# A new order of the opening transfers: value weights in two transfers on SyncE's queue, the head map on ScalarE's

## The chip, the cores and the metric

The kernel runs on one core of a Trainium2 chip. The metric is the time of one execution in microseconds (us) of device time. The profile also gives a span, from the first to the last counted instruction; it is somewhat shorter than the time. SyncE, ScalarE (ACT) and GpSimd (POOL) issue transfers (DMAs); VectorE is DVE, TensorE is PE. "Landing" is the moment at which the last of a transfer's 16 completions is in, so that an instruction that waits for it may go (in the kernel before x's second half landed at 6.22 us, and the product that waited for it started at 6.27). Three runs of the kernel before gave 148.55 us as the median.

## The reference

The function mixes two blocks over x (2048 rows of 448, bf16), row by row, with a gate.

```python
g = sigmoid((x * gate_w).sum(-1, keepdims=True))
a = A(x)   # linear attention, 16 heads of 28: qkv = x @ wqkv; a head map w_phi on q and k,
           # softmax of it and of its negative; kv = phi_k^T v; o = phi_q kv / (phi_q z); o @ wo
b = B(x)   # gelu(x @ w1 + b1) @ w2 + b2, hidden size 1792
return g * a + (1 - g) * b
```

The kernel multiplies the head map into the key and query weights first ("fuse", tile `w_ps`), so that a key goes from x to its features in one product. That fuse needs the key weights transposed, and the map.

## The kernel before

Only the opening matters here. Transfers are issued in the order of these lines, each on the queue of the engine that is named:

```python
nc.vector.memset(warm[:], 0.0)
nc.vector.memset(wphi[HP:P, 3, :], 0.0)          # the map's unused rows alone (HP = 64, P = 128)
nc.vector.memset(gb[:], 0.0); nc.vector.memset(bb[:], 0.0)
nc.sync.dma_start(x0[:, 0:2, :], two[0])         # x, first half of its first 512 rows, 224 KB
nc.scalar.activation(out=tiny[:, 0:1], in_=warm[0:1, 0:1], func=ACT.Exp)
nc.scalar.dma_start(WvG[:, 0:3, 0:D], A_wqkv[0:384, 2 * D:3 * D].rearrange("(c p) n -> p c n", p=P))   # 336 KB
wflat = A_w_phi.rearrange("h a b -> (h a) b")
nc.sync.dma_start(wphi[:, 0:3, :], wflat[0:384, :].rearrange("(c p) b -> p c b", p=P))   # 21 KB
nc.scalar.dma_start(wphi[0:HP, 3, :], wflat[384:448, :])                                 # 3.5 KB
nc.sync.dma_start(x0[:, 2:4, :], two[1])         # x, second half, 224 KB
# ... GpSimd: the last 64 rows of the value weights twice (2 x 56 KB), gate weights, ...
load_wT(WkT, D, 0, 256)                          # key weights, transposing transfers on SyncE
load_wT(WkT, D, 256, D)
```

TensorE meanwhile runs filler products, turns x (`tp`), and multiplies by the value weights (`v_ps`):

```python
idle(5); idle(6, P)                              # fillers (w_warm)
turn(0, 1, nc.vector.tensor_copy, 0, 2)          # needs x's first half
turn(0, 2, nc.scalar.copy, 2, 4)
turn(2, 0, nc.vector.tensor_copy)
idle(2, P)
v0a, v0b = V(0, 3), V(1, 0)
v0a.un.full(0, True, False)                      # 3 products, one for each value chunk of 128 rows
v0a.un.full(1, True, False, cs=(0,))
# ... then the turns and products of x's second half, then the fuse of the key weights
```

The softmax here doesn't subtract the row's maximum and nothing guards it: scores larger than these inputs give would overflow.

## Time and profile before

| Kernel before | |
|---|---|
| time, span | 148.78 us and 147.1 us in the profiled run |
| x's first half: issue, landing | 0.80, 3.43 us |
| value weights (one transfer) | 0.96, 4.67 us |
| x's second half | 1.73, 6.22 us |
| key weights, two transposes: landing | 7.12, 8.44 us |
| first product of the key fuse (`w_ps`) | 8.33 us |

The page's first part says how busy each engine is; TensorE, at 97%, is the bound, so a change in the opening acts by when TensorE can run through without a hole. The moment that sums the opening up is the start of the first `w_ps` product, 8.33 us: from there to the end of the span it takes 138.8 us (147.1 - 8.33). The prediction below shows the lines of this profile with the chain of waits and the timeline up to 6.9 us. Two further lines of TensorE's timeline are needed for comparison (start, length, engine, line, operation, output and inputs, shape, count):

```profile
6.72 1.77 PE L194 MATMUL v_ps<-gel,xT 128*128 128x448 bf16 x8
8.33 0.63 PE L316 MATMUL w_ps<-gel 128*128 128x140 bf16 x8
```

Eight products of 448 columns take 1.77 us, and the fuse follows; single products of 448 columns start 0.19 us apart in the instruction records.

### The profile page before, as it was taken

What the parts mean: (1) busy time and instruction counts of PE and PEld (TensorE: products, weight loads), DVE (VectorE), ACT (ScalarE), POOL (GpSimd) and SP (SyncE); (2) the same over time, 40 slices, a digit from 0 to 9 for tenths busy, and PEclk for the clock granted to TensorE, in tenths of its full rate; (3) what the DMA queues carried; (4) which work ended last, traced back from release to release, by engine and by line L of the source; (5) the groups of instructions that cost most, each with busy time, mean ns of one, the idle gap of its engine ahead of it and who ended that gap; (6) DMA issues with size and microseconds to landing.
All of it is one profiled execution on the core that took longest, in us unless ns stands there. A gap on an engine that the chain in (4) does not pass through costs nothing.

```text
span 147.1 us, 3117 instructions
## 1 busy us (share of the span) xinstructions
PE 142.9 (97%) x1293; PEld 78.5 (53%) x1293; DVE 82.5 (56%) x140; ACT 64.8 (44%) x73; POOL 72.0 (49%) x59
## 2 busy tenths in 40 slices
PE   7899999999999999999999999999999999999992
PEld 4554645554566666964444445554555555545561
DVE  0342999997999992179993002721637747044112
ACT  4266987889999877326777762000000000000000
POOL 7932499898889999200699940000621110024000
PEclk9999999999999999999999999999999999999999
DMA  4999857449999999997159990340313623303111
GB/s 129 266 184 224 199 123 150 108 85 241 224 221 223 366 246 145 181 153 139 38 98 171 100 206 0 71 76 2 125 31 85 87 69 71 71 4 125 60 34 31
DMA packets 46190, 18.98 MB, mean 129 GB/s; under 512 B 36800, under 2 KB 46016, under 8 KB 46176
## 3 DMA queue, kind: packets, MB, share of 16 engines
q1 hardware_dynamic: 45392, 18.23, 61.8%
q10 hardware_dynamic: 624, 0.43, 0.9%
q8 instruction: 10, 0.16, 0.5%
q0 software_dynamic: 160, 0.12, 0.3%
q14 instruction: 4, 0.03, 0.1%
HBM read 6.34 MB, written 1.84 MB: 56 GB/s over the span
## 4 chain that ended last, share of the span: by engine, by line
PE 94%; DMA 3%; SPq 1%; DVE 0%; issue 0%
PE hp L478 29%; PE y L577 28%; PE q_ps L231 6%; PE y L194 6%; PE k_ps L231 4%; PE v_ps L194 3%; DMA gel<-in_A_x_dram 3%; PE v_ps L231 3%; PE kv L490 3%; PE nm L502 2%; PE k_ps L205 2%; PE k_ps L194 2%; PE w_ps L316 1%; PE y L211 1%; PE q_ps L194 1%; PE v_ps L211 1%
## 5 line engine op out<-in xcount | busy, mean ns | idle before, releaser
L577 PE MATMUL y<-w_sb,gel 128*128 128x448 bf16 (+1 forms) x224 | 43.8, 349 | 0.0
L478 PE MATMUL hp<-xT,w_sb 64*128 64x512 bf16 x224 | 42.7, 376 | 0.0
L478 PE MATMUL hp<-xS,w_sb 64*128 64x512 bf16 x168 | 40.1, 376 | 0.0
L482 ACT ACTIVATE gel<-hp,b1T 128x1024 bf16<-128x1024 f32 x28 | 30.8, 1115 | 13.6 <-PE hp L478 13.0
L478 PEld LDWEIGHTS <-w_sb 64*128 64x128 bf16 x392 | 22.9, 94 | 19.1
L577 PEld LDWEIGHTS <-gel 128*128 128x128 bf16 x238 | 22.3, 98 | 19.3 <-issue 0.4
L538 POOL TENSOR_SCALAR b2u<-b2b,ungate 128x448 f32<-128x448 bf16 x16 | 10.0, 642 | 40.2 <-DVE res L589 40.2
L259 POOL TENSOR_TENSOR gel<-gel,rec 128x1792 bf16<-128x1792 bf16 x8 | 25.6, 3214 | 2.2 <-DVE rec L258 2.2
L589 DVE SCALAR_TENSOR_TENSOR res<-y,ungate,b2u 128x448 bf16<-128x448 f32 (+1 forms) x16 | 10.3, 673 | 25.0 <-PE y L577 13.2
L259 POOL TENSOR_TENSOR phiq<-phiq,rec 128x1792 bf16<-128x1792 bf16 x4 | 12.7, 3211 | 11.0 <-DVE rec L258 11.0
L256 DVE TENSOR_REDUCE sums<-gel 128x64 f32<-128x1792 bf16 x8 | 16.0, 2002 | 0.0
L250 ACT ACTIVATE gel<-k_ps 128x896 bf16<-128x896 f32 x16 | 13.7, 922 | 3.5 <-PE k_ps L231 2.1
L509 DVE TENSOR_SCALAR den<-nm,enL 128x16 f32<-128x16 f32 x16 | 3.6, 228 | 17.0 <-PE nm L502 17.0
L231 PEld LDWEIGHTS <-xT 64*128 64x128 bf16 x112 | 9.2, 94 | 5.6 <-issue 0.4
L259 POOL TENSOR_TENSOR phqT<-phqT,rec 128x1792 bf16<-128x1792 bf16 x3 | 11.3, 3808 | 0.0
L515 DVE TENSOR_TENSOR o_all<-nm,den 128x448 bf16<-128x448 f32 (+2 forms) x24 | 11.0, 485 | 0.6
L231 PE MATMUL q_ps<-gel,xT 64*128 64x448 bf16 (+1 forms) x56 | 10.1, 349 | 0.0
L231 PEld LDWEIGHTS <-xS 64*128 64x128 bf16 x84 | 7.8, 94 | 3.8
L258 DVE RECIPROCAL rec<-sums 128x64 f32<-128x64 f32 x16 | 8.9, 553 | 1.1
L231 PE MATMUL q_ps<-phqT,xS 64*128 64x448 bf16 (+1 forms) x42 | 9.1, 349 | 0.0
L278 DVE CAST vaug<-v_ps 128x896 bf16<-128x896 f32 x7 | 7.5, 1070 | 2.7 <-PE v_ps L194 2.4
L194 PE MATMUL y<-wo_sb,phiq 128*128 128x448 bf16 (+1 forms) x36 | 8.2, 349 | 0.0
(96 smaller groups left out, 146.4 us busy)
## 6 DMA issues: line engine op xcount, KB each, us to landing
w_sb<-in_B_w_dram SPq DMA_DIRECT2D x4, 784.0 KB, 10.8
out_dram<-res SPq DMA_DIRECT2D x15, 112.0 KB, 1.7
w_sb<-in_B_w_dram SPq DMA_DIRECT2D x2, 560.0 KB, 13.6
xS<-xT SPq DMA_DIRECT2D x8, 96.0 KB, 2.3
phqT<-gel SPq DMA_DIRECT2D x4, 168.4 KB, 3.4
gel<-in_A_x_dram SPq DMA_DIRECT2D x2, 224.0 KB, 3.6
w_sb<-in_B_w_dram SPq DMA_DIRECT2D x1, 448.0 KB, 10.2
gel<-in_A_wqkv_dram ACTq DMA_DIRECT2D x1, 336.0 KB, 3.7
```

The source lines that it names most:

```text
L194: nc.tensor.matmul(o, lhsT=self.L(i, slice(0, P), c), rhs=self.R(slice(0, P), c)[:, n0:n1], start=(first and c == 0), stop=(last and c == 2))
L231: nc.tensor.matmul(o, lhsT=tok, rhs=(W if direct else SWAPPED[name])[rows, c, 0:n], start=(k == 0), stop=own)
L250: nc.scalar.activation(out=o, in_=src, func=ACT.Exp, scale=(1.0, -1.0)[s])
L256: nc.vector.reduce_sum(out=sums[:], in_=ph, axis=AX.X)
L258: nc.vector.reciprocal(out=rec[:], in_=sums[:])
L259: eng.tensor_tensor(out=ph, in0=ph, in1=rec[:, :, :, None].to_broadcast([P, 32, 2, DH]), op=ALU.mult)
L478: nc.tensor.matmul(hp[:, i, :].rearrange("p (b t) -> p b t", b=2), lhsT=w1_sb[i * HP:(i + 1) * HP, k, j * P:(j + 1) * P], rhs=x_half(i, k, ...
L482: nc.scalar.activation(out=dst, in_=hp[:].rearrange("p i (b t) -> p i b t", b=2), func=ACT.Gelu_apprx_tanh, bias=b1T[:, j:j + 1])
L515: nc.vector.tensor_tensor(out=o_tok[:, col:col + (b - a) * DH].rearrange("p (q j d) -> p q j d", j=2, d=DH), in0=nm[:, a // 2:b // 2, 0:56 ...
L538: nc.gpsimd.tensor_scalar(out=b2u[t][:], in0=b2b[:], scalar1=ungate[:, place(t):place(t) + 1], scalar2=0.0, op0=ALU.mult, op1=ALU.add)
L577: nc.tensor.matmul(o, lhsT=gel[:, j, tok], rhs=w2_sb[:, j, n0:n1], start=(first and j == 0), stop=(last and j == NJ - 1))
L589: nc.vector.scalar_tensor_tensor(out=res[t][:, n0:n1], in0=o, scalar=ungate[:, e:e + 1], in1=b2u[t][:, n0:n1], op0=ALU.mult, op1=ALU.add)
```

## The change

Its intent is to have the first value chunk sooner and to let x's and the value weights' bytes flow from one queue in the order in which TensorE wants them, with the small packets of the map out of the way on ScalarE's queue.

```diff
     nc.vector.memset(warm[:], 0.0)
-    nc.vector.memset(wphi[HP:P, 3, :], 0.0)
     nc.vector.memset(gb[:], 0.0)
     nc.vector.memset(bb[:], 0.0)
+    nc.vector.memset(wphi[:], 0.0)
     nc.sync.dma_start(x0[:, 0:2, :], two[0])
     nc.scalar.activation(out=tiny[:, 0:1], in_=warm[0:1, 0:1], func=ACT.Exp)
-    nc.scalar.dma_start(WvG[:, 0:3, 0:D], A_wqkv[0:384, 2 * D:3 * D].rearrange("(c p) n -> p c n", p=P))
+    for c0, c1 in ((0, 1), (1, 3)):
+        nc.sync.dma_start(WvG[:, c0:c1, 0:D],
+                          A_wqkv[c0 * P:c1 * P, 2 * D:3 * D].rearrange("(c p) n -> p c n", p=P))
+    nc.sync.dma_start(x0[:, 2:4, :], two[1])
     wflat = A_w_phi.rearrange("h a b -> (h a) b")
-    nc.sync.dma_start(wphi[:, 0:3, :], wflat[0:384, :].rearrange("(c p) b -> p c b", p=P))
+    nc.scalar.dma_start(wphi[:, 0:3, :], wflat[0:384, :].rearrange("(c p) b -> p c b", p=P))
     nc.scalar.dma_start(wphi[0:HP, 3, :], wflat[384:448, :])
-    nc.sync.dma_start(x0[:, 2:4, :], two[1])
 ...
-    for c0, c1 in ((0, 1), (1, 3)):
-        nc.sync.dma_start(wo_sb[:, c0:c1, :], A_wo[c0 * P:c1 * P, :].rearrange("(c p) n -> p c n", p=P))
+    nc.sync.dma_start(wo_sb[:, 0:3, :], A_wo[0:384, :].rearrange("(c p) n -> p c n", p=P))
```

The output weights in one transfer are a side effect: the number of transfers stays what it was.

## The prediction

> **What bounds the kernel now.** I read the page's first part first, then the chain of waits in order of time, then the timeline of the first 14 us, and last the landings of the transfers that the change touches.
>
> ```profile
> PE 142.9 (97%) x1293; PEld 78.5 (53%) x1293; DVE 82.5 (56%) x140; ACT 64.8 (44%) x73; POOL 72.0 (49%) x59
> ```
>
> TensorE is busy 142.9 of 147.1 us. Whatever the change does, it can only take from the 4.2 us in which TensorE is idle, or add to them. The chain in order of time says where those lie in the part that the change touches:
>
> ```profile
> 0.74 0.06 issue
> 0.80 0.41 SPq L116
> 1.21 0.06 issue
> 1.27 0.41 SPq L120
> 1.68 0.05 issue
> 1.73 4.49 DMA gel<-in_A_x_dram
> 6.22 0.05 issue
> 6.27 0.62 PE tp L336 x8
> 6.88 1.61 PE v_ps L194 x8
> ```
>
> The columns are start, length in us and what it was. The chain begins with three issues on SyncE (x's first half, the head map wphi, x's second half), then the flight of x's second half from 1.73 to 6.22 us, and from 6.27 us on it is TensorE piece by piece until the end. So the whole kernel starts at the landing of x's second half; what comes later or sooner at 6.22 us moves the end one for one, as long as no other transfer takes over. The timeline on TensorE shows how long it waits there:
>
> ```profile
> 3.57 1.06 PE L336 MATMUL tp<-ident,gel 128*128 128x128 bf16 x8
> 4.42 0.42 PE L322 MATMUL w_warm<-const-bfloat16-1.0 128*128 128x128 bf16 x2
> 4.89 0.93 PE L194 MATMUL v_ps<-gel,xT 128*128 128x448 bf16 x4
> 6.27 0.62 PE L336 MATMUL tp<-ident,gel 128*128 128x128 bf16 x8 [0.44 <-DMA gel<-in_A_x_dram]
> ```
>
> The page's idle is 0.44 us, from the modelled end of the fourth value matmul. In the instruction records these matmuls start 0.19 us apart (5.09, 5.28, 5.47), so the next one could have started at 5.66: the real hole before x's second half is 6.27 - 5.66 = 0.61 us. That is one limit of a gain. There is a second, smaller hole: the last filler starts at 4.53, fillers are 0.107 us apart, and the first value matmul comes at 4.89 instead of 4.63. The value weights landed at 4.67 and TensorE's sequencer ended its wait at 4.70, so 0.26 us are lost to the value weights. But that hole is in front of the wait for x's second half, so closing it only makes the later hole longer.
>
> [...] the value weights on ScalarE's queue had the engines between x's first and second half, with packets from 2.77 to 4.10 us, and SyncE's queue almost stood still meanwhile. [...] x's first half (issued 0.80) has its packets from 1.83 to 3.09, the value weights (0.96) from 2.77, the map (1.27) from 3.83 to 4.27, the map's last rows (1.43) from 4.00 to 4.51, x's second half (1.73) from 4.03 to 5.42. Over two queues they come in the order of their issue. [...] Here x's first half takes 1.03 us from issue to its first packet, and x's second half 0.80 us from its last packet's end to its landing at 6.22: 1.8 us together[...].
>
> **The change part by part.** Issues on SyncE cost 0.41 to 0.48 us, and the next follows 0.05 us later. Before: x first half at 0.80, map 1.27, x second half 1.73, key transposes 2.25. After: x first half 0.80, first value chunk 1.27, the other two 1.73, x second half about 2.19 (0.46 later), key transposes about 2.7 (0.45 later). ScalarE issued the value weights at 0.96 and now has only the two map transfers, behind VectorE's fill of the whole map. That fill is now the fourth memset on VectorE, which ended its four at 1.31 before; so the map is issued at about 1.4 and 1.9.
>
> (a) Order on the DMA engines. What goes ahead of x's second half is the same before and after: 224 KB of x, 336 KB of value weights, 24.5 KB of map, only in another order. The map is 448 packets of 56 B at a mean of 11 ns: 448 x 11 ns / 16 engines = 0.3 us, wherever it stands. All the hardware queues' data goes out from 1.83 us with the engines busy from 2.5 us on (share 0.8 to 1.1 in the windows)[...]. x's second half issued at 2.19 could, by the 1.03 us of the first half, have packets at 3.2; the engines reach it at 4.0. So the 0.46 us on SyncE lie wholly beside the queue. I expect its landing at 6.2, plus or minus 0.3. The difference is worth 0.
>
> (b) The first value chunk (112 KB, a third) lands sooner, by perhaps 0.5 us. The 0.26 us hole before the value matmuls closes, and reappears in front of x's second half. Worth 0. The other chunks may land slightly later than 4.67, up to about 4.9; also before that wait. Worth 0.
>
> (c) The map: needed by VectorE at 7.04, landed at 4.96 and 5.39 before. With issue at 1.4 and 1.9 it has 1.5 us to spare or more. The larger fill adds about 0.1 us on VectorE at 1.2 us, where it sits idle until 4.02. Worth 0.
>
> (d) The key transposes are issued 0.45 us later. Their packets began at 5.01, when x's second half had gone, so the first stays queue-bound; it landed at 7.12, its matmuls start at 8.33. The second landed at 8.44 and its first user is at 9.37: if it takes all 0.45 us it lands at 8.9, still in time. The later transposes:
>
> ```profile
> 2.25 2.79 SPq L125 DMA_TRANSPOSE gel<-in_A_wqkv_dram  x2
> 5.09 2.94 SPq L129 DMA_TRANSPOSE xT<-in_A_x_dram  x1
> 8.08 1.64 SPq L125 DMA_TRANSPOSE gel<-in_A_wqkv_dram  x1
> 9.76 3.27 SPq L129 DMA_TRANSPOSE xT<-in_A_x_dram  x1
> 13.16 3.42 SPq L141 DMA_DIRECT2D phqT<-gel  x4
> ```
>
> These follow one another without a wait, so all slip by 0.45 us. x's next block landed at 10.88 and GpSimd's copy of it ends at 11.41, used at 12.97; the query weights landed at 13.16, copied by 13.68, used at 15.54; x's third block landed at 16.72, used at 19.5. Slack 1.5 us or more each. SyncE's own waits then swallow the slip:
>
> ```profile
> SPq L141 <- DVE gel L410: 1.2, 1, 1.2
> ```
>
> SyncE waits 1.2 us for VectorE before 19.29, so from there it runs on its old times. Worth 0.
>
> (e) The output weights in one transfer in place of two: one issue of about 0.5 us less at 33.7 us, in a stretch where SyncE afterwards waits on semaphores anyway, and used only past 80 us. Worth 0.
>
> Sum: 148.55 + 0, with the landing of x's second half as the one term that can differ. I put in -0.05 for the chance that it gains from no longer standing behind the map in its own queue: 148.5 us.
>
> **The rivals.** First: x's second half lands sooner. Its 16 completions came in two bunches, 5.51 to 5.67 and 6.03 to 6.22, with the engines nearly still between:
>
> ```profile
> 5.50:5.75 0.25, 0.25 (x2) 0.00 (x0) 0.00 (x0) 0.00 (x0) 0.25 (x1) 1.00 2.07 217
> 5.75:6.00 0.25, 0.07 (x1) 0.00 (x0) 0.00 (x0) 0.00 (x0) 0.25 (x1) 1.00 0.35 34
> ```
>
> The last two numbers are DMA share and GB/s. If another order misses this stall of about 0.4 us, the landing is near 5.8 and the time 148.1; with 0.26 us more from the closed hole, the limit is some 0.6 to 0.9 us, so 147.7. Against: the bytes ahead are the same. Second: x's second half lands later, because its issue, 0.46 us later, does bind or because the map now interleaves with it: at most 0.46 us, 149.0. Against: the first-packet estimate leaves 0.8 us of room. Third: a new wait on the second key transpose, if it slips more than its 0.93 us of slack, as transposes came 2.7 us or more from issue to first packet; each further tenth costs a tenth. I expect 0.
>
> **Range and chances.** The rivals give -0.6 to +0.5 around 148.55, each unlikely at its full size, and the three runs of before already span 0.5 us. So 148.0 to 149.1. Two per cent is 2.97 us: more than all TensorE idle at stake in this opening, so faster by over 2% would need more than what is there, and slower would need a wait that no slack above allows.
>
> **What would show it.** Right: in the chain, the flight of x's second half still ends at about 6.2, now from an issue at about 2.2; the idle before the second transposes grows from 0.44 to about 0.7 (the closed hole moved); value matmuls start near 4.65; key-transpose issue at about 2.7; no wait of TensorE on the key weights. Wrong: x's second half landing before 5.8 or after 6.6, value matmuls that wait for the second chunk transfer beyond 5.2, or a TensorE wait on the key transposes at 8 to 9.5 us.

## The result, and the profile after

The changed kernel took 150.82 us as the median of six runs (150.05 to 151.45), against 148.72 us for the kernel before in six runs (148.32 to 149.05). The ratio is 1.0137, with a 95% interval of 1.0097 to 1.0178. Ratios here and below are the mean time of one kernel's runs over that of the other's of the same rounds, so they are not quite the ratio of the medians quoted. The kernel is slower, and 150.82 lies outside the predicted 148.0 to 149.1.

The six times form two groups: 150.05, 150.32 and 150.45, and 151.20, 151.21 and 151.45. The profile is of the slowest, 151.45 us. First its engines' busy times:

```profile
PE 144.4 (97%) x1293; PEld 75.2 (50%) x1293; DVE 82.4 (55%) x140; ACT 64.7 (43%) x73; POOL 72.0 (48%) x59
```

TensorE has the same 1293 instructions and is busy 144.4 us instead of 142.9. More busy time for the same work means slower products, not only longer waits. The chain of waits in order of time (start, length, what it was) of the changed kernel:

```profile
0.80 0.41 SPq L116
...
1.27 0.41 SPq L119
...
1.73 4.91 DMA gel<-in_A_wqkv_dram
6.64 0.04 issue
6.68 1.28 PE v_ps L196 x3
7.96 0.85 PE tp L338 x8
8.82 2.00 PE v_ps L196 x8
10.82 0.46 PE w_ps L318 x8
```

Before, the flight in this chain was that of x's second half, until 6.22. Now it is the second transfer of value weights (chunks 1 and 2, 224 KB): issued at 1.73, landed only at 6.64. TensorE's timeline shows the same from the other side:

```profile
4.42 0.42 PE L324 MATMUL w_warm<-const-bfloat16-1.0 128*128 128x128 bf16 x2
4.90 0.53 PE L196 MATMUL v_ps<-gel,xT 128*128 128x448 bf16 x1
6.68 1.28 PE L196 MATMUL v_ps<-gel,xT 128*128 128x448 bf16 x3 [1.26 <-DMA gel<-in_A_wqkv_dram]
7.76 1.06 PE L338 MATMUL tp<-ident,gel 128*128 128x128 bf16 x8
8.61 2.21 PE L196 MATMUL v_ps<-gel,xT 128*128 128x448 bf16 x8
10.66 0.63 PE L318 MATMUL w_ps<-gel 128*128 128x140 bf16 x8
```

There are two things to see. TensorE does one value product at 4.90 and then waits 1.26 us for the second transfer. And what follows is slow: three value products take 1.28 us (four took 0.93 before), eight transposes 1.06 (0.62 before), eight value products 2.21 (1.77 before). The records have single products of 448 columns 0.373 us apart instead of 0.189, and transposes 0.107 us instead of 0.056, until about 9.6 us: half pace. The fuse then starts at 10.66 us instead of 8.33, 2.33 us later, and the rest takes 138.7 us, as before. So the whole difference of the spans, 149.4 - 147.1 = 2.3 us, is made before that product.

| | before | after |
|---|---|---|
| first value chunk landed | 4.67 (one transfer) | 3.80 |
| all value weights of SyncE or ScalarE landed | 4.67 | 6.64 |
| x's second half: issue, landing | 1.73, 6.22 | 2.20, 7.24 |
| map, first and last part landed | 4.96, 5.39 | 3.99, 6.38 |
| key transposes landed | 7.12, 8.44 | 8.59, 9.88 |
| first `w_ps` product | 8.33 | 10.66 |

The engines' busy times by stretch (start and end, length, busy time and instructions of PE, PEld, DVE, ACT and POOL, granted clock, DMA share, GB/s) tell why the second transfer is late. First the kernel before, then the changed one:

```profile
3.25:4.25 1.00, 1.00 (x12) 1.00 (x11) 0.23 (x1) 0.02 (x1) 1.00 (x3) 1.00 1.18 319
```

```profile
3.25:4.25 1.00, 1.00 (x12) 0.93 (x11) 0.23 (x1) 0.01 (x1) 1.00 (x3) 1.00 0.72 121
```

In this microsecond the DMA engines moved 319 GB/s before and 121 GB/s after, though the second value transfer had been issued at 1.73 us and x's second half at 2.20. In the packet records the value weights come at 66 and 42 packets of 896 B in the quarters of a microsecond from 2.75 and 3.0, which by their count are the 128 of the first chunk, and then, for the second transfer, at 30, 21, 12 and 16; from 4.5 to 5.25 the engines carry 300 GB/s or more again. I call this the trickle. About 0.2 MB were not moved in it, which is 0.6 us at 319 GB/s (an estimate from the two rates: 198 GB/s less for 1 us).

The 0.6 us are not the whole delay of x's second half, which comes to 1.02 us. Packets of 256 B, by their time those of the key transposes, begin at 5.09 us and share the engines with x's last packets of 1792 B, which end at 6.85; before, they began at 5.01, and x's ended at 5.42. How much of the rest this makes is not measured.

The difference of the two profiled runs then has three terms.

1. x's second half lands 1.02 us later (7.24 against 6.22).
2. From that landing to the fuse it takes 10.66 - 7.24 = 3.42 us instead of 8.33 - 6.22 = 2.11 us: 1.31 us more at half pace.
3. The time exceeds the span by 151.45 - 149.4 = 2.05 us, against 148.78 - 147.1 = 1.68 before: 0.37 us lie outside the span.

The sum is 1.02 + 1.31 + 0.37 = 2.70 us, and the measured difference is 151.45 - 148.78 = 2.67. It is an account with x's landing as its mark, and not the chain itself: in this run the value weights released TensorE at 6.64, and with three value products at half pace it came to the transposes at 7.76, when x's second half (7.24) had been in for 0.5 us. For the faster group of runs (mean 150.27 us) the first and third term alone make 148.72 + 1.39 = 150.1, if x's second half landed there as in the profiled run, which no trace shows.

### The profile page after: what moved, and what is told of

Its sections match the earlier page's.

```text
span 149.4 us, 3117 instructions
## 1 busy us (share of the span) xinstructions
PE 144.4 (97%) x1293; PEld 75.2 (50%) x1293; DVE 82.4 (55%) x140; ACT 64.7 (43%) x73; POOL 72.0 (48%) x59
## 4 chain that ended last, share of the span: by engine, by line
PE 94%; DMA 3%; SPq 1%; DVE 0%; issue 0%
PE hp L479 28%; PE y L578 28%; PE q_ps L233 6%; PE y L196 6%; PE v_ps L196 5%; PE k_ps L233 4%; DMA gel<-in_A_wqkv_dram 3%; PE v_ps L233 3%; PE kv L491 2%; PE nm L503 2%; PE k_ps L207 2%; PE k_ps L196 2%; PE w_ps L318 1%; PE y L213 1%; PE q_ps L196 1%; PE v_ps L213 1%
## 5 line engine op out<-in xcount | busy, mean ns | idle before, releaser
L479 PE MATMUL hp<-xS,w_sb 64*128 64x512 bf16 x168 | 40.7, 376 | 0.0
L479 PEld LDWEIGHTS <-w_sb 64*128 64x128 bf16 x392 | 18.8, 94 | 23.2
L196 PE MATMUL v_ps<-gel,xT 128*128 128x449 bf16 (+1 forms) x30 | 7.9, 401 | 1.3 <-DMA gel<-in_A_wqkv_dram 1.3
```

The lines of the kernel that those rows point to most:

```text
L196: nc.tensor.matmul(o, lhsT=self.L(i, slice(0, P), c), rhs=self.R(slice(0, P), c)[:, n0:n1], start=(first and c == 0), stop=(last and c == 2))
L479: nc.tensor.matmul(hp[:, i, :].rearrange("p (b t) -> p b t", b=2), lhsT=w1_sb[i * HP:(i + 1) * HP, k, j * P:(j + 1) * P], rhs=x_half(i, k, ...
```

## The experiments

Seventeen kernels ran; all gave correct results. Times are medians, with the kernel before on the same chip beside them. Landings and starts are of the one profiled run. The theories that the expectations name by letters are these. M: the map's small packets on ScalarE's queue take the DMA engines from the value weights. S: it is the split of the value weights. G: it is the two 56 KB transfers on GpSimd's software queue that disturb. D: it is the place in the queue, the value chunks being the third transfer that SyncE puts in. D1 and D2 are two mechanisms for D. F: the fill of the whole map costs time outside the span.

### The map

e1_map_sp_last: the changed kernel with the large map transfer on SyncE behind x's second half.

```diff
-    nc.scalar.dma_start(wphi[:, 0:3, :], ...)
+    nc.sync.dma_start(wphi[:, 0:3, :], ...)
```

> The changed kernel, but the map's first 384 rows go out on SyncE behind x's second half; only the map's last 64 rows stay on ScalarE. Theory M (the map's small packets on ScalarE's queue, in flight beside the value chunks on SyncE's, hold the chunks up): the other value chunks land by 5.0 us, x's second half by 6.4, time 148.3 to 149.0. Rival Q (value chunks are slow because they share SyncE's queue with x, map or no map): chunks still land after 6 us, time 150 or more. Rival S (the split into two value transfers): as Q here, 150 or more.

Measured: 150.02 us (149.98 to 151.36) against 148.69, ratio 1.0109 (1.0065 to 1.0154). Value chunks landed at 6.45, x's second half at 7.14 us. The trickle is there (90 GB/s in the stretch 3.25:4.25) with only the map's last 64 rows, 3.5 KB, on the other queue.

e2_map_late: the changed kernel with the fill and both map transfers moved behind the copy of the first x block (issued at 4.41 and 6.82 us).

```diff
-    nc.vector.memset(wphi[:], 0.0)                # and both map transfers, from the opening
     turn(0, 1, nc.vector.tensor_copy, 0, 2)
+    nc.vector.memset(wphi[:], 0.0)
     turn(0, 2, nc.scalar.copy, 2, 4)
+    nc.scalar.dma_start(wphi[:, 0:3, :], ...)
+    nc.scalar.dma_start(wphi[0:HP, 3, :], ...)
```

> The changed kernel, but the map's fill stands behind VectorE's first copy out of PSUM, so both map transfers are issued at 4.4 us or later, after the value chunks should be through. Theory M: other value chunks land by 5.0 us, x's second half by 6.4; the map may come late for VectorE at 7.0 to 7.5, so 148.3 to 149.5. Rivals Q and S: chunks land after 6 us, 150 or more.

Measured: 151.69 us (151.38 to 151.94) against 148.69, ratio 1.0199 (1.0177 to 1.0222). Value chunks at 6.80, x's second half at 7.49 us, fuse at 11.18. With no map at all in the first 4.4 us the chunks come no sooner. Theory M is out. This kernel is slower for a further reason as well, half pace again (the first product of the fuse comes 3.7 us after x's landing), and its map lands at 10.62, so its time is not read further.

e4_before_map_act: the kernel before, with the large map transfer on ScalarE behind the value weights.

```diff
-    nc.sync.dma_start(wphi[:, 0:3, :], ...)
+    nc.scalar.dma_start(wphi[:, 0:3, :], ...)
```

> The kernel before, with one line changed: the map's first 384 rows on ScalarE behind the value weights instead of on SyncE ahead of x's second half. Value weights stay on ScalarE's queue in one transfer. Theory M in its wide form (small packets on one hardware queue slow large ones on the other): the map now runs beside x's second half, which lands later than 6.2, 149 or more. M in its narrow form (only when the map reaches the engines before the value chunks are through) and Q: x's second half lands at 5.7 to 6.2, time 148.1 to 148.7.

Measured: 148.41 us (148.08 to 148.88) against 148.69, ratio 0.9982 (0.9954 to 1.0010). x's second half, now second on SyncE, landed at 5.46 us instead of 6.22, and yet the fuse started at 8.26. So a sooner x wasn't worth its 0.76 us. Here the first value products took it: they start at 4.89 at half pace, 0.37 us apart, and TensorE comes to the second transposes only at 6.21. In e13 below, the same kernel once more, these products ran at full pace and the key weights took over: they landed at 8.21 us, and the fuse, after a wait for them, began at 8.26. The map on ScalarE does no harm.

### One transfer or two

e3_one_chunk: the changed kernel with the value weights in a single transfer, still on SyncE (the output weights split again).

```diff
-    for c0, c1 in ((0, 1), (1, 3)):
-        nc.sync.dma_start(WvG[:, c0:c1, 0:D], ...)
+    nc.sync.dma_start(WvG[:, 0:3, 0:D], A_wqkv[0:384, 2 * D:3 * D].rearrange("(c p) n -> p c n", p=P))
```

> The changed kernel with the value weights as one transfer on SyncE, and the output weights in two again, so that the number of transfers stays. Theory M: the map still runs beside the value weights, so they land after 6 us and the time stays at 150 or more. Rival S: landing by 5.0 us, 148.3 to 149.0. Rival Q: 150 or more.

Measured: 148.85 us (148.83 to 149.09) against 148.69, ratio 1.0015 (0.9996 to 1.0034). The value weights landed at 4.67, x's second half at 5.95, the fuse started at 8.05. The stretch that showed the trickle, in this kernel:

```profile
3.25:4.25 1.00, 1.00 (x15) 0.89 (x13) 0.29 (x1) 0.18 (x1) 1.00 (x3) 1.00 1.19 326
```

It carries 326 GB/s. The same bytes on the same queue with one issue fewer have no trickle. But this changes two things at once: the number of transfers, and that the last value bytes are second on SyncE and no longer third. The span is 146.7 us, 0.4 us less than before's, and the time nevertheless no shorter; e15 to e17 come back to that.

e5_before_split_act: the kernel before with the value weights in two transfers on ScalarE, and the output weights in one.

```diff
-    nc.scalar.dma_start(WvG[:, 0:3, 0:D], ...)
+    for c0, c1 in ((0, 1), (1, 3)):
+        nc.scalar.dma_start(WvG[:, c0:c1, 0:D], A_wqkv[c0 * P:c1 * P, 2 * D:3 * D]...)
```

> The kernel before, with its value weights on ScalarE in two transfers (first chunk, other two) and the output weights in one, nothing else changed. Theory S (the early boundary between two value transfers is what costs, whatever the queue): the other chunks land after 5.5 us, 149.7 or more. Rival SQ (the split costs only where the chunks share a queue with x): the other chunks land by 5.0 us and the time is within 0.4 of before.

Measured: 149.69 us (runs 148.79, 148.96, 150.43 and 150.73) against 148.69, ratio 1.0071 (1.0007 to 1.0134). Of the 16 completions of the second transfer 15 were in by 4.64 us, one straggled until 5.96; the fuse came at 10.20 us in a profiled run (150.73 us) with half pace. So a split alone, with its second transfer second in ScalarE's queue, made no trickle here, but the straggler and the two groups of times leave the case against S unfinished; the time is inconclusive.

### GpSimd's queue

e6_tails_act moves GpSimd's two value transfers to ScalarE behind the map; e7_tails_late issues them on GpSimd after the gate weights.

```diff
     for i in range(2):
-        nc.gpsimd.dma_start(WvG[i * HP:(i + 1) * HP, 3, 0:D], A_wqkv[384:448, 2 * D:3 * D])
+        nc.scalar.dma_start(WvG[i * HP:(i + 1) * HP, 3, 0:D], A_wqkv[384:448, 2 * D:3 * D])   # e6
```

> The changed kernel, but the last 64 rows of the value weights (two transfers of 56 KB) leave GpSimd's software queue and go out on ScalarE behind the map. Theory G (at the boundary after the first chunk the DMA engines turn to the software queue, whose packets of 3584 B took 0.3 to 1 us each there, against 0.14 to 0.2 in the kernel before, and the chunks wait behind them): with no such packets the other chunks land by 5.2 us, x's second half by 6.5, time 148.3 to 149.2. Rival B (the boundary itself stalls, no matter what else is queued): other chunks after 5.5 us, 149.7 or more.

> The changed kernel, but GpSimd issues the two 56 KB transfers behind its two small gate transfers, about 2 us later. Theory G: the other chunks land by 5.2 us and x's second half by 6.5; but the late rows may land at 8 to 9 us, when TensorE needs them at 8.9, so 148.3 to 149.8. Rival B: other chunks after 5.5 us, 149.7 or more.

Measured: e6 151.11 us (150.02 to 152.27) against 148.69, ratio 1.0165 (1.0098 to 1.0232), chunks at 5.83 and x at 6.74. e7 151.05 us (149.75 to 151.21), ratio 1.0136 (1.0083 to 1.0190), chunks at 5.97 and x at 6.63. The chunks remain more than a microsecond behind 4.67, and the time doesn't fall. In e7 the first packet of GpSimd's two transfers moves at 6.83 us, and the stretch of the trickle carries even less than in the changed kernel:

```profile
3.25:4.25 1.00, 1.00 (x12) 1.00 (x11) 0.23 (x1) 0.01 (x1) 1.00 (x2) 1.00 0.65 72
```

G is not the cause. That the chunks landed some half a microsecond sooner than in the changed kernel can't be put down to these packets: e8 below has the transfers of the changed kernel unaltered, and its one profile shows 244 GB/s in this stretch and the chunks at 5.73. So far does the trickle differ from run to run.

### The place in the queue

e9_c0_act: chunk 0 on ScalarE ahead of the map, so that chunks 1 and 2 are second on SyncE.

```diff
-    for c0, c1 in ((0, 1), (1, 3)):
-        nc.sync.dma_start(WvG[:, c0:c1, 0:D], ...)
+    for c0, c1, eng in ((0, 1, nc.scalar), (1, 3, nc.sync)):
+        eng.dma_start(WvG[:, c0:c1, 0:D], ...)
```

> The changed kernel with only the first value chunk moved to ScalarE, ahead of the map; SyncE carries x's first half, the other two chunks, x's second half. The boundary between the two value transfers stays, but no queue has a large transfer as its third. Theory D (the third transfer put into one queue early on is held until the first one's completion is back, at 3.0 to 3.5 us, and about 1 us more): the other chunks are second here, land by 5.0 us, x's second half by 6.3, time 148.1 to 149.0. Rival B (any early boundary between the two value transfers stalls): the other chunks land after 5.5 us, 149.7 or more.

Measured: 149.27 us (149.15 to 149.34) against 148.89, ratio 1.0027 (1.0012 to 1.0042). Chunks 1 and 2 landed at 4.87, x's second half at 5.80 us, fuse at 8.26, span 147.1, and 323 GB/s in the stretch 3.25:4.25: still two transfers, and no trickle. This is the case against S that e5 could not make. With the first chunk moved to ScalarE the other two landed at 4.87 instead of 6.64 us (5.73 in e8), though their issue came only 0.46 us sooner. It isn't the number of issuers that does it: in e3 x and all value weights are issued on SyncE, the value weights second, and they landed at 4.67.

e10_c12_first: both on SyncE, in the other order.

```diff
-    for c0, c1 in ((0, 1), (1, 3)):
+    for c0, c1 in ((1, 3), (0, 1)):
```

> The changed kernel with its two value transfers swapped on SyncE: the other two chunks second in the queue, the first chunk third. Theory D: the other chunks, now second, land by 4.6 us, and the small first chunk, now third, is the one that trickles and lands after 5.0 us; time 149 to 150.5. Rival P (the shape of the two-chunk transfer is slow wherever it stands): the two-chunk transfer lands after 5.5 us again. If neither is late, the early boundary was the cause: 148.3 to 149.

Measured: 149.19, 149.28, 149.61 and, slow, 151.77 us, median 149.44, against 148.89; ratio 1.0037 (1.0009 to 1.0064). Chunks 1 and 2, now second, landed at 4.30 us; chunk 0, now third and only 112 KB, at 5.55. What was late before is early now, and the other way round: it is the place, not the shape. The delay is milder here (277 GB/s in the stretch 3.25:4.25; the larger transfer ahead flows until about 3.7 us), and so is the loss of time, of which the fill makes 0.35 us (see "Outside the span").

e11_one_chunk_third: e3 (one value transfer) with the map's last 64 rows, 3.5 KB, put on SyncE between x's first half and the value weights, so that the single transfer is third.

```diff
+    nc.sync.dma_start(wphi[0:HP, 3, :], wflat[384:448, :])
     nc.sync.dma_start(WvG[:, 0:3, 0:D], ...)
     nc.sync.dma_start(x0[:, 2:4, :], two[1])
-    nc.scalar.dma_start(wphi[0:HP, 3, :], wflat[384:448, :])
```

> The kernel of the single value transfer on SyncE, but with the map's last 64 rows (3.5 KB) put between x's first half and the value weights on SyncE, so that the value weights are third in the queue. Theory D: the value weights are held and land after 5.2 us, time 149.5 or more. Rival B (splitting the value weights is what costs): they land by 5.0 us, time 148.6 to 149.1.

Measured: 151.88 us (151.74 to 152.16) against 148.89, ratio 1.0206 (1.0187 to 1.0224). One 3.5 KB transfer ahead moved the landing of the value weights from 4.67 to 6.64 us, x's second half to 7.36, the fuse to 11.14. Of the 1.97 us of the first, 0.62 are the later issue (1.88 for 1.26); counted from the issue the landing took 4.76 us instead of 3.41. The stretch and TensorE's waits of this kernel (engine, tile and line, what it waited for; total, times, longest us):

```profile
3.25:4.25 1.00, 1.00 (x12) 1.00 (x11) 0.23 (x1) 0.02 (x1) 1.00 (x3) 1.00 0.89 84
```

```profile
PE v_ps L194 <- DMA gel<-in_A_wqkv_dram: 2.1, 1, 2.1
```

It carries 84 GB/s, and TensorE waits 2.1 us for the value weights. With the split gone and the trickle back, this settles place against the split. x's first half landed at 3.40 us, as in the kernel before. The DMA share of 0.89 is no contradiction to the few bytes: GpSimd's packets of 3584 B took 0.82 us on average from 3.2 to 3.9 us (0.26 to 1.63), and most of them 0.14 us later on.

e12_tiny_first asks what lies beneath. The 3.5 KB are now first on SyncE, x's first half second, the value weights third (with before's fill). If a queue held its third transfer until the first was complete (D1), the tiny first one, complete at 2.79 us, would free it early.

```diff
+    nc.sync.dma_start(wphi[0:HP, 3, :], wflat[384:448, :])
     nc.sync.dma_start(x0[:, 0:2, :], two[0])
     nc.sync.dma_start(WvG[:, 0:3, 0:D], ...)
```

> Single value transfer on SyncE as third again, but the small transfer (the map's last 64 rows) now stands first in the queue, ahead of x's first half, and so completes by about 2.9 us. Theory D1 (the third waits for the first one's completion): the value weights flow right behind x's first half, whose landing moves from 3.4 to about 3.9 with its later issue, and land by 5.3 us; time 148.9 to 149.5. Theory D2 (the third is late by its position, each transfer taking the queue about 1 us to get under way, completion or not): value packets start at 4 us or later, they land after 6 us, 151 or more.

Measured: 149.64, 149.64, 151.14 and 151.34 us, median 150.39, against 148.68; ratio 1.0138 (1.0097 to 1.0180). The value weights, issued at 2.06, had first packets at 3.63, trickled until 4.5, and landed at 6.24 us. D1, with a landing by 5.3, fell. D2 had the landing right and neither the start of the packets nor the time. What the runs give is a description: the third transfer of the queue sends a few packets and comes to its full rate 2.4 to 2.9 us after its issue (from about 4.5 us on for an issue at 1.73 in the changed kernel, 4.75 for 1.88 in e11, 4.5 for 2.06 here). The first transfer, x's first half, issued at 0.80, was at its full rate from 2.5 us on, 1.7 us after its issue (387 GB/s from 2.50 to 2.75 in the changed kernel).

Over all 19 profiles: the value weights, or the last two chunks of them, landed at 5.73 to 6.80 us in the nine kernels that have them third on SyncE (the changed kernel, e1, e2, e6, e7, e8, e11, e12, e17), and at 4.67 to 4.96 in the eight that have them first or second in their queue (before, e3, e4, e9, e13 to e16); e5 with its straggler is the exception, and in e10 they are parted. Counted from their issue on SyncE, it is 4.00 to 5.08 us as third and 3.41 to 3.60 as second (e3, e9, e15). The third were also issued later, at 1.72 to 2.06 us against 0.96 to 1.27; a later issue without the third place was not tried. The mechanism stays open.

### The half pace

e8_after_fill: the changed kernel with five filler products of 512 columns between the first value product and the second.

```diff
-    v0a.un.full(0, True, False)
+    v0a.un.full(0, True, False, cs=(0,))
+    w_warm = pair("w_fill", slot=2)
+    idle(5)
+    v0a.un.full(0, True, False, cs=(1, 2))
     v0a.un.full(1, True, False, cs=(0,))
```

> The changed kernel with five more filler matmuls of 512 columns on TensorE between the first value matmul and the second, where it waits idle from about 5.3 to 6.6 us. Theory C (of the loss some 1.4 us is TensorE at half pace, because its idle wait kept it from its full pace until about 9.6 us): matmuls at 0.19 us pitch by 7.5 us, time 149.5 to 149.9. If only the late landing counts: no change or a little slower, 150.3 to 151.

Measured: 150.07 us (149.57 to 150.55) against 148.69, ratio 1.0093 (1.0061 to 1.0126): between the two ranges that were expected. TensorE's timeline of its profiled run (149.57 us, the fastest of four):

```profile
4.49 1.25 PE L324 MATMUL w_fill<-const-bfloat16-1.0 128*128 128x512 bf16 x5
5.77 0.73 PE L196 MATMUL v_ps<-gel,xT 128*128 128x448 bf16 x3
7.19 1.77 PE L196 MATMUL v_ps<-gel,xT 128*128 128x448 bf16 x8
```

Three value products in 0.73 us and eight in 1.77: full pace, and from x's landing (6.68) to the fuse (8.79) 2.11 us, as in the kernel before. In e1, e3 and e6 too, where TensorE was at full pace after x's landing, this stretch is 2.10 to 2.11 us; among the profiles at half pace it is 3.42 (the changed kernel), 3.53 (e7), 3.69 (e2), 3.73 (e17), 3.78 (e11) and 4.07 (e5). So the size of the term is measured. That the fillers bring it about is not proved: the chunks also landed sooner in e8's profile (5.73 us), TensorE was at full pace in it before the fillers came, and e1 had full pace after an idle stretch nearly as long as the changed kernel's (one value product at 4.89, the next at 6.49 us), without fillers. Whether the hole brings half pace differs from run to run. This fits the two groups of times, though only one run of each kernel has a trace here.

The traces also hold records of the granted clock, and these say what the half pace is. In e11 it shows in the view (three stretches that end where a record does; the 1.00 or 0.50 before the DMA share is the granted clock):

```profile
4.36:7.77 3.41, 1.30 (x14) 0.79 (x12) 0.42 (x1) 0.25 (x1) 3.41 (x5) 1.00 1.13 259
7.77:11.18 3.41, 3.41 (x16) 1.64 (x14) 1.25 (x5) 0.59 (x1) 0.96 (x2) 0.50 1.06 199
11.18:14.59 3.41, 3.41 (x32) 2.02 (x31) 1.62 (x2) 2.45 (x5) 0.39 (x1) 1.00 0.91 168
```

TensorE was idle for 2.11 us of the first stretch, in the next it had half the clock, though it was busy throughout (eight value products from 8.15 us on took 3.18 us, against 1.77 in the kernel before), and then the full clock again. e2 has the same (idle 1.91 us, half clock from 7.58 to 10.99). In the kernel before the records begin with the full clock at 4.96 us, in the changed one at 9.68, where the products come to full pace. Counted back from there in steps of 3.41 us, the length of the half-clock stretches of e2 and e11 (an estimate, as the changed kernel has no earlier record), it had such a stretch from 2.86 to 6.27, and in it the hole, 0.90 us of it; the full clock did not come at its end but one step later. In e1 the full clock came at 5.28, before most of the hole, and with 1.08 us idle in the next stretch it stayed. By these records, holes of nearly one size cost nothing or some 1.3 us, by where they fall. This is read from records of single runs, and no experiment moves the hole alone.

The clock records can begin late (at 9.68 us in the changed kernel), and the granted clock of a stretch before the first record reads 1.00 (6.27:9.68 there) though the products of 448 columns in it run at half pace, 0.373 us apart; there the pace is to be read from the distance of equal products.

### Outside the span

Each run lists time and span. In all kernels with the fill of the whole map the difference was 2.03 to 2.14 us (in e2 too, where the fill runs only at 4.28); in those with before's fill 1.67 to 1.79. Three kernels change the fill alone. e15_one_chunk_oldfill is e3 with before's fill, e16_before_wholefill is the kernel before with the fill of the whole map, e17_after_oldfill the changed kernel with before's fill.

```diff
-    nc.vector.memset(wphi[HP:P, 3, :], 0.0)
     nc.vector.memset(gb[:], 0.0)
     nc.vector.memset(bb[:], 0.0)
+    nc.vector.memset(wphi[:], 0.0)      # e16; e15 and e17 the other way round
```

> One value transfer on SyncE (second in its queue), as in e3, but with the fill of before (last 64 rows alone), so that the first map transfer doesn't wait for VectorE. In e3 the span was 146.7 us, 0.4 us shorter than before's, and the time equal; in all kernels with the whole-map fill the time exceeds the profiled span by about 2.1 us, in those with before's fill by about 1.7 us. Theory F (the whole fill, or the wait for it, costs about 0.35 us outside the span): span 146.6 to 146.9, time 148.2 to 148.6, 0.997 to 1.000 of before. Rival (the difference between time and span has to do with the value weights on SyncE): span as in e3, time 148.8 to 149.1.

> The kernel before with nothing changed but the fill: the whole map instead of its last 64 rows, so that SyncE's map transfer waits for VectorE. Theory F: span 147.0 to 147.3, time minus span 2.0 to 2.2 us, time 149.0 to 149.3 (1.002 to 1.004). Rival: time minus span stays at 1.7, time within 0.1 us of before.

> The changed kernel with before's fill. Position theory: value chunks 1 to 2 still third on SyncE, land at 6.0 to 6.7, x's second half at 6.7 to 7.3. Theory F: time 0.3 to 0.4 us less than the changed kernel, 150.2 to 150.6, time minus span 1.7. Rival: 150.7 to 151.0, time minus span 2.1.

Measured, against 148.54 us for the kernel before: e16 149.01 us (148.85 to 149.40), ratio 1.0023 (1.0009 to 1.0036), time less span 2.05 to 2.11 us in all five runs, with a median span of 146.9 us against 146.8. So the fill alone costs about 0.35 us (0.0023 x 148.5 = 0.34), and shows nowhere in the profile. e15 took 148.85 us (148.55 to 149.18), ratio 1.0012 (0.9997 to 1.0028): time less span fell to 1.68 to 1.78 us, as F has it, but the span was 147.0 us in the profile instead of e3's 146.7, because x's second half landed at 6.20; the time of 148.2 to 148.6 that F asked for did not come. e17 took 148.58, 149.45 and 149.78 us in three runs and 151.18 to 151.33 in three that are slow, being over 1.5% above the fastest (ratio of the fast ones 1.0042, 1.0012 to 1.0072). Its time less span was 1.68 to 1.75 us, as F has it. Its profile, of a slow run, has the chunks at 6.50 and x at 7.15 us. As to time e17 is inconclusive; one of its runs, with a span of 146.9 us, must have escaped the trickle or nearly so, which no trace shows.

F holds in all three for the difference, and in e16 for the time. What it is that costs the 0.35 us is open: the memset itself takes 0.10 us instead of 0.07.

### Is there a version that beats both?

e13_map_act_again repeats e4 in five rounds, e14_map_act_nofill is e4 without the two fillers ahead of the value products.

```diff
-    idle(2, P)                          # e14
```

> The kernel before with the map on ScalarE behind the value weights, once more with five rounds: x's two halves are first and second on SyncE, the value weights first on ScalarE. Theory D: 148.2 to 148.7 again, 0.1 to 0.3 % below before; noise would put it at before.

> As e13, without the two filler matmuls that stand in front of the value matmuls (0.107 us each). The value weights land at 4.68 us either way, so the first value matmul can start at about 4.75 instead of 4.89: 0.1 us less than e13 if TensorE comes to full pace at the same time, 0.2 to 0.5 us more if the missing fillers put that off.

Measured: e13 148.76 us (148.42 to 148.79) against 148.68, ratio 1.0002 (0.9989 to 1.0016); the gain of 0.1 to 0.3% that was expected did not show. e14 148.57 us (148.24 to 149.97), ratio 1.0007 (0.9977 to 1.0037); its slowest run is the profiled one, whose fuse starts at 8.08 us, so it lost its time later in the kernel. No version beat the kernel before.

## Why the prediction was wrong

**What bounds the kernel** was right in the main: TensorE piece by piece from the opening's last landing on, and what comes later there moves the end one for one. But the change could do more than "take from the 4.2 us in which TensorE is idle, or add to them": TensorE's busy time itself grew by 1.5 us at half pace. The remainder after the first fuse product was 138.7 to 138.8 us before, after, and in e1, e3, e8 and e11.

**Step (a), order on the DMA engines, is the step that failed.** It said that "x's second half issued at 2.19 could, by the 1.03 us of the first half, have packets at 3.2; the engines reach it at 4.0", and made the difference worth 0. The 1.03 us were taken from the first transfer of a queue and used for later ones. (The prediction's "1.8 us together" likewise adds the start of x's first half to the tail of its second; the first half alone has 1.03 us and, from 3.09 to 3.43, 0.34 us.) The bytes ahead of x's second half were the same, as the step had it, but they didn't flow: the transfer in third place trickled until about 4.5 us. The issues themselves came when the step said (2.20). x's second half landed at 7.24 instead of "6.2, plus or minus 0.3": a term of 1.02 us.

The kernel before has a third transfer on SyncE too, x's second half itself. There it cost next to nothing in time: with x second on SyncE (e4) it landed 0.76 us sooner, and the fuse began 0.07 us sooner. ScalarE's value weights kept the engines busy from 2.77 to 4.10 us. The prediction saw that "SyncE's queue almost stood still meanwhile" and read it as the engines being taken; with all bulk transfers but GpSimd's on SyncE's queue nothing filled that time (121 GB/s in the stretch 3.25:4.25, against 319 before).

**Step (b)**: the first chunk landed 0.87 us sooner (3.80 against 4.67), more than the 0.5 us that it said. The hole did not close: the first value product came at 4.90, after fillers at half pace. "The other chunks may land slightly later than 4.67, up to about 4.9" was the worst miss, 6.64; it rests on the same assumption as (a), and in the profiled run it is the wait on which TensorE's chain hangs.

**Step (c)**: the large part of the map landed at 3.99, sooner than before, and the map was no cause (e1, e2). But "the larger fill ... Worth 0" was wrong by 0.35 us outside the span (e16), which no reading of spans could have shown.

**Step (d)**: issue at 2.71 as said. The second key transpose landed at 9.88 instead of 8.9, with x's packets under way until 6.85; no wait of TensorE on it showed, since everything before it was late too. **Step (e)**: nothing pointed to the output weights; they were not tested alone.

**The rivals.** The second had the direction, a later landing of x, and a limit of 0.46 us that came from the issue alone; measured 1.02. None had TensorE at half pace: the sum treats a hole as its own length, and TensorE, at half pace when the hole before the second value product came, was still at half pace after it, which made 1.31 us more in the profiled run. The clock records point to the hole (see e8); no experiment shows it by itself. The list of what would make it wrong named the two signs that came: value products waiting beyond 5.2 for the second transfer, and x's second half after 6.6.

**The range** took its width from the repeated times of before and the rivals, not from the untested assumption in (a), on which every part of the sum rested. Its failure was worth 1.02 us directly, and opened the hole behind which TensorE ran at half pace.

## What to carry to other kernels

Before bulk transfers are gathered on one queue, look at when the second, third and fourth transfer of a queue send their packets, not only at the first: here the third came to its full rate 2.4 to 2.9 us after its issue, the first 1.7 us, and in the kernel before two queues side by side hid it (319 GB/s in the stretch 3.25:4.25, against 121). Where a hole of a microsecond opens in front of TensorE early in a kernel, reckon with the products behind it at half pace: 1.3 us more in the changed kernel's profile, nothing in e1's. And compare times as well as spans: a fill of 0.1 us cost 0.35 us where the profile shows nothing.
